# Rooms handed out by age, weights narrowed ahead, sums on VectorE and a first pair split from PSUM, in an attention kernel with two MLPs

## The chip, the cores and the metric

The kernel runs on one core of one Trainium2 chip. The metric is the device time of one execution in microseconds (us); lower is better. Five engines work side by side: TensorE (PE, matmuls), VectorE (DVE), ScalarE (ACT), GpSimd (POOL) and SyncE (SP), which here only starts DMA transfers. Each engine works through its own instructions in program order and waits where an operand isn't there yet.

## The reference

```python
scores = scale * q @ k.T - log(S)            # 4 batches, 12 heads, S = 448, head width 64
x = sigmoid(scores) @ v                      # attention without a row sum
x = x.transpose(0, 2, 1, 3).reshape(1792, 768)
h = x @ w_in                                 # layer 0: 768 -> 2048 -> 768
x = where(h > 0, h, exp(min(h, 0)) - 1) @ w_out
h = x @ w_in2                                # layer 1, same sizes
out = (h - tanh(h)) @ w_out2
```

The weights arrive as 64-bit floats. They are read as pairs of 32-bit integers and narrowed on the chip to 32-bit floats.

## The kernel before, in words

**Precision.** Each matmul operand is split into a rounded high part (`hi`, or a "head") and what is left (`lo`, or a "rest"), and each product is made of three matmuls: high by high, high by rest, rest by high. A head is one copy on ACT (or DVE), a rest one subtraction on DVE.

**Attention.** 24 pairs of heads go through two at a time ("n" is the pair, "m" the two). For a pair, q and k are loaded, POOL lays them side by side (`side`, L254; the first two pairs are loaded in that layout), PE transposes them (`t`), ACT and DVE copy the result from PSUM (`plain`, L352 and L354), DVE or ACT makes `hi` and DVE `lo` in the tile `e` (L366, L370), PE forms the scores (`s`, L389), ACT the sigmoids (`sig`, L410), PE the product with v (`pv`, L416). Beside it the second weights of layer 0 are loaded, narrowed (`p_load`, `p_narrow`, L617 to L624), summed and stored to memory.

**MLP layers.** Layer i is two Strassen products in the Winograd form with seven block products P1 to P7. A step (i, g, s) is the g-th of eight groups of hidden columns and half s of the rows (512 or 384 wide). For each (i, g) two tiles of `w_in` are loaded to `first` and `second` and narrowed by three instructions (ACT, DVE, DVE); four block sums S1, S2, S4, S3 are formed (`w_sum`, L737), and then heads and rests (`w_head` L751 on ACT, `w_rest` L754 on DVE). The places W0 to W3 hold them: W0 is for P1 and P2, W1 (from S1 and S2) for P5 and P6. Between step (i, g-1, 1) and (i, g, 0) lies what is called passage (i, g) here. In a step, ACT copies P1, P5 and P6 out of PSUM (`snap` s1, s5, s2, L834), DVE adds the rest (`h_add`, L839), ACT and DVE form the activation (`g_a`, `g_b`, `g_c`) and DVE the sums for the next product (`g_sum`, L884), and SP stores the seven forms (`f_store`, L888). `first_out` (layer 0) and `strassen_out` (layer 1) form the second product: they load the forms back (`og_load`, L946) and the weights' forms (`ow_load`, L935), split them (L949, L953, L938, L942), and multiply (L977) in the order P1, P5, P6, P3, P7, P2, P4. During `first_out` the second weights of layer 1 are loaded and narrowed in the rooms R1a and R1b in turn and kept in memory (`ahead`; L606, L617 to L624, L632). At the end of `first_out`, R1a and R1b also take up the layer's output (`o2_out`, L995).

**Rooms.** Snaps, activations and loaded forms stand in numbered rooms t0 to t25, parts of the tiles `t`, `second`, `spare`, `R1b` and others. `ring` gives out the room of a list that was given out longest ago, as the program is written, and a user waits until the former users are done:

```python
slot_of[key] = t = min(slots, key=lambda t: (used.get((kind[0], t), 0), slots.index(t)))
used[kind[0], t] = turns[0]
```

The lists are in `RINGS`: "g0" for the loads of `first_out` (rooms 23 to 25, then 0 to 6), "s10" for the snaps of steps (1, 0, s=0), "s11" for s=1, "sa" for step (0, 0, 1).

**Order.** PE's order in the MLP part is written out (`sequence`). The other engines' order is planned while the program is built, in `Sched`: of the ready operations the one that can start first by the planner's costs comes next, then the one with the lower rank (`when` for attention, from `PHASES`, `SHIFTS` and `FIRST_PAIRS`; for the rest the time at which PE wants it). So an edit of a cost, a dependence or a rank also moves operations that it doesn't name. In the opening, `ld_first` loads q and k of pairs 0 and 1, `ld_v` v; `loads` says which come first.

Of the kernel before, what the change touches and what calls it, by code (L numbers as in the profile page):

```python
# [121 lines left out]
SHIFTS = {(0, "ldv"): -12000, (0, "sr"): ROUND - 4700, (0, "sigr"): ROUND - 3900, (0, "ldvr"): -11000}  # L122
# [4 lines left out]
def kernel(  # L127
# [20 lines left out]
    nc = tc.nc  # L148
# [46 lines left out]
    with tc.manual_schedule():  # L195
# [7 lines left out]
        def attention():  # L203
# [59 lines left out]
            def ld_first(kind, i):  # L263

                b, hp = pairs[i]
                h = slice(2 * hp, 2 * hp + 2)
                if kind == "k":
                    nc.sync.dma_start(out=kl[:, i].rearrange("p c (h d) -> p c h d", h=2), in_=k[b, h, 0:KW].rearrange("h (p c) d -> p c h d", c=3))
                else:
                    (nc.sync if i else nc.scalar).dma_start(out=ql[:, i].rearrange("p c (h d) -> p c h d", h=2), in_=q[b, h].rearrange("h (p r) d -> p r h d", r=R))  # L270

            def ld_v(m, i0, i1):
                by = nc.sync if i1 == NL else nc.scalar
                b, hp = pairs[NL * m]
                by.dma_start(
# [13 lines left out]
            def loads(m):  # L289
# [8 lines left out]
                fns = {"ldv": ld_v, "ldkr": lambda m: ld_rests(0, m), "ldvr": lambda m: ld_rests(1, m), "ldkfirst": lambda i: ld_first("k", i), "ldqfirst": lambda i: ld_first("q", i)}  # L298
                for x, key in enumerate(todo):
# [5 lines left out]
                    sch.moves[key] = {"ldv": 650 * (args[-1] - args[-2]) if kind == "ldv" else 0, "ldkr": 290, "ldvr": 290, "ldkfirst": 630, "ldqfirst": 740}[kind]  # L305
# [3 lines left out]
            def loaded(kind, n):  # L309
# [3 lines left out]
                part = [("side", n, w) for w in range(2)] if m else [("ldkfirst", i), ("ldqfirst", i)]  # L313
# [29 lines left out]
            def drain(n, x):  # L343
                by, lo, hi = parts_of(n)[x]
                at = DD * (n % 2)
# [16 lines left out]
            def hi(n):  # L362
                if hi_on(n) == "ACT":
# [95 lines left out]
            for n in range(NPR):  # L459
# [12 lines left out]
                for y, (by, c0, c1) in enumerate(parts_of(n)):  # L472
                    op(("plain", n, y), by, int(1.06 * (c1 - c0)) + 120 if by == "DVE" else int(0.83 * (c1 - c0)) + 190, drain, [("t", n), ("sr", m - 1), ("lo", n - 2)])
                op(("hi", n), hi_on(n), 600 if hi_on(n) == "DVE" else 880, hi, drained(n) + [("s", n - 2, u) for u in range(3)])
                op(("lo", n), "DVE", 1020, lo, [("hi", n)])
# [15 lines left out]
        def mlp():  # L491
# [247 lines left out]
            def sum_on(step):  # L739
                return "DVE" if step == (0, 0) else "POOL"  # L740
# [509 lines left out]
            def first_products(step):  # L1250
# [14 lines left out]
                kind, kind_r = ("sa" if step == (0, 0, 1) else f"s1{s}", "r1") if g == 0 else ("s2", "r")  # L1265
# [222 lines left out]
            for i in range(2):  # L1488
# [4 lines left out]
                for g in range(NG):  # L1493
                    first_weights(i, g)
                    for s in range(2):
                        first_products((i, g, s))
                        if (i, g, s) == (0, 0, 1):
# [66 lines left out]
```

## Time and profile before

| | us |
|---|---|
| timed runs: median of 3 | 983.35 (983.11 to 986.51) |
| the profiled execution's own time | 987.84 |
| its span, first to last instruction | 985.8 |
| PE busy in it | 969.9 |
| DVE, ACT, POOL busy | 762.4, 610.3, 107.8 |

The profile is that of one execution. Its span is what the trace shows, and some 2 us lie around it. In the views below, a row of the timeline is an instruction or a run of like ones: its start, its length, engine, line, operation, "output tile <- input tiles", shape and count, and in brackets the idle time of the engine before it with what ended that. A row of the waits sums such idle time by what was waited for.

### The profile page before, as it was taken

Reading aid. Unit: us, or ns where it says so; the run is one execution under the profiler, and the core shown is the slowest. Engines: PE = TensorE matmul, PEld = TensorE weight load, DVE = VectorE, ACT = ScalarE, POOL = GpSimd, SP = SyncE. Lnnn points to the kernel's source line nnn. Section 1 sums busy time; section 2 is a strip of 40 time slices with the busy share of each in tenths; the row PEclk is TensorE's granted clock in tenths of the full one; section 3 lists DMA queues with packets and bytes.
Section 4 is the critical chain, followed back from the end, with each engine's and each line's share of the span. In section 5 each row is a group of like instructions: output and inputs, shape, how many; then the busy total and the mean of one; then the engine's idle time right before and its main releaser. Section 6 shows DMA issues by size and latency. Waiting matters only on the chain.

```text
span 985.8 us, 15460 instructions
## 1 busy us (share of the span) xinstructions
PE 969.9 (98%) x5306; PEld 837.6 (85%) x5306; DVE 762.4 (77%) x1110; ACT 610.3 (62%) x951; POOL 107.8 (11%) x110
## 2 busy tenths in 40 slices
PE   8999999999999999999999999999999999999998
PEld 5545556989999997888999987899888999999998
DVE  3877998988888886688887997877777897656673
ACT  5889889666666675566666563444444575446652
POOL 2222311011111100000000201111111000000000
PEclk9999999999999999999999999999999999999999
DMA  8999970465555599999956525555554994455442
GB/s 244 328 318 324 329 267 17 163 211 180 189 191 189 191 303 384 381 375 375 366 173 216 162 72 189 184 186 193 195 181 158 350 318 143 131 163 177 128 143 82
DMA packets 144575, 218.61 MB, mean 222 GB/s; under 512 B 21424, under 2 KB 102896, under 8 KB 144240
## 3 DMA queue, kind: packets, MB, share of 16 engines
q1 hardware_dynamic: 143232, 217.10, 64.8%
q8 instruction: 41, 0.67, 0.3%
q10 hardware_dynamic: 1264, 0.52, 0.2%
q14 instruction: 38, 0.31, 0.1%
HBM read 142.61 MB, written 74.97 MB: 221 GB/s over the span
## 4 chain that ended last, share of the span: by engine, by line
PE 93%; DMA 3%; DVE 2%; ACT 1%; SPq 1%; issue 1%; POOL 0%; DVEq 0%; ACTq 0%; POOLq 0%
PE psa L822 13%; PE psd L822 12%; PE psx L822 10%; PE psu L977 6%; PE psv L977 6%; PE psw L977 6%; PE psa L977 6%; PE psb L977 6%; PE psb L822 6%; PE pv L416 5%; PE psy L977 5%; PE sps L389 4%; PE psx L977 3%; PE psd L977 1%; DMA R1a<-in_moe_w_in_dram 1%; PE pv L427 1%
## 5 line engine op out<-in xcount | busy, mean ns | idle before, releaser
L949 ACT ACTIVATE XB<-t 128x384 fp32r<-128x384 f32 (+1 forms) x111 | 62.5, 563 | 40.0 <-PE psw L977 12.2
L953 DVE TENSOR_TENSOR XB<-t,XB 128x384 fp32r<-128x384 f32 (+1 forms) x111 | 68.4, 626 | 12.6 <-ACT XB L949 12.1
L737 POOL TENSOR_TENSOR second<-second 128x384 f32<-128x384 f32 x15 | 17.7, 1180 | 549.3 <-DMA t<-x_forms 212.5
L410 ACT ACTIVATE an<-sps,bias 128x896 f32<-128x896 f32 x72 | 70.7, 1024 | 9.7 <-PE sps L389 9.2
L949 ACT ACTIVATE XB<-spare 128x512 fp32r<-128x512 f32 (+1 forms) x72 | 41.0, 572 | 27.2 <-PE psw L977 9.6
L416 PE MATMUL pv<-an,vl 128*64 128x448 f32 x288 | 56.8, 544 | 0.0
L822 PE MATMUL psa<-XB,W 128*128 128x512 f32 x192 | 55.2, 396 | 0.0
L389 PE MATMUL sps<-e 64*128 64x448 f32 x432 | 52.5, 380 | 1.1 <-ACT plain L352 0.7
L389 PEld LDWEIGHTS sps<-e 64*128 64x128 f32 x432 | 37.6, 184 | 16.9 <-issue 7.8
L416 PEld LDWEIGHTS pv<-an,vl 128*64 128x64 f32 x288 | 19.5, 136 | 36.5 <-issue 30.7
L953 DVE TENSOR_TENSOR XB<-spare,XB 128x512 fp32r<-128x512 f32 (+1 forms) x72 | 44.1, 621 | 7.8 <-ACT XB L949 7.7
L254 POOL COPY first<-raw_qk 128x384 f32<-128x384 f32 (+1 forms) x44 | 36.4, 852 | 93.8 <-DMA raw_qk<-in_k_dram 74.2
L977 PE MATMUL psu<-XB,XB 128*128 128x384 f32 (+1 forms) x192 | 46.3, 348 | 0.0
L977 PE MATMUL psv<-XB,XB 128*128 128x384 f32 (+1 forms) x192 | 46.2, 348 | 0.0
L977 PE MATMUL psw<-XB,XB 128*128 128x384 f32 (+1 forms) x192 | 46.2, 348 | 0.0
L822 PEld LDWEIGHTS psa<-XB,W 128*128 128x128 f32 x192 | 36.8, 192 | 7.9
L851 ACT ACTIVATE spare<-t 128x512 f32<-128x512 f32 (+1 forms) x33 | 19.1, 579 | 37.0 <-DVE t L839 35.9
L822 PE MATMUL psd<-XB,W 128*128 128x512 f32 x144 | 36.8, 399 | 2.6 <-DVE W L754 2.4
L855 ACT ACTIVATE spare<-spare 128x512 f32<-128x512 f32 (+1 forms) x64 | 36.7, 576 | 1.4
L977 PE MATMUL psa<-XB,XB 128*128 128x384 f32 (+1 forms) x156 | 36.8, 347 | 0.0
L977 PE MATMUL psb<-XB,XB 128*128 128x384 f32 (+1 forms) x156 | 36.8, 347 | 0.0
L977 PEld LDWEIGHTS psu<-XB,XB 128*128 128x128 f32 x192 | 34.7, 188 | 2.1 <-DVE XB L942 0.2
(370 smaller groups left out, 2724.1 us busy)
## 6 DMA issues: line engine op xcount, KB each, us to landing
x_forms<-R1b SPq DMA_DIRECT2D x58, 256.0 KB, 2.0
first<-p_forms SPq DMA_DIRECT2D x36, 384.0 KB, 6.6
t<-x_forms SPq DMA_DIRECT2D x64, 192.0 KB, 2.9
t<-x_forms SPq DMA_DIRECT2D x47, 256.0 KB, 5.3
x_forms<-t SPq DMA_DIRECT2D x45, 256.0 KB, 2.0
x_forms<-R1b SPq DMA_DIRECT2D x58, 192.0 KB, 2.0
first<-in_moe_w_in_dram SPq DMA_DIRECT2D x14, 768.0 KB, 5.8
second<-in_moe_w_in_dram SPq DMA_DIRECT2D x14, 768.0 KB, 5.2
```

What stands on the lines that cost most here:

```text
L254: nc.gpsimd.tensor_copy(out=(ql, kl)[w][:, n % NL].rearrange("p c (h d) -> p c h d", h=2), in_=x)
L389: nc.tensor.matmul(out=ps[:, j, :S], lhsT=e[lanes, EW * kz + u * 128:EW * kz + (u + 1) * 128], rhs=e[lanes, EW * qz + KW:EW * qz + EW], st ...
L410: nc.scalar.activation(out=a, in_=T.pop(("s", n, u))[:, :, :S], func=ACTF.Sigmoid, bias=bias, scale=scale)
L416: nc.tensor.matmul(out=T["o", n][D * j:D * j + D, :S], lhsT=vl[m % NVL][:, x, 3 * j + u], rhs=a[:, j], start=False, stop=(u == 2), skip_gr ...
L427: nc.tensor.matmul(out=T["o", n][D * j:D * j + D, :S], lhsT=vrest[n // NR % 2][lanes, m % (NR // 2), j], rhs=a[lanes, j], start=True, stop ...
L737: by.tensor_tensor(out=out, in0=x, in1=y, op=op)
L822: nc.tensor.matmul(out=ps, lhsT=w[wz][:, k0:k0 + 128], rhs=xs[xz][:, kk], start=(opens and n == 0), stop=(n == 3 * KH - 1), skip_group_che ...
L851: nc.scalar.activation(out=r, in_=h, func=ACTF.Tanh)
L855: nc.scalar.activation(out=r, in_=r, func=ACTF.Exp, scale=-1.0)
L949: nc.scalar.activation(out=at_place(og_place[i, s, p, j], 0, i)[:, :HW[s]], in_=T["graw", i, s, p, j], func=ACTF.Copy)
L953: nc.vector.tensor_tensor(out=lo, in0=T.pop(("graw", i, s, p, j)), in1=f(hi), op=ALU.subtract)
L977: nc.tensor.matmul(out=T["o2", tag], lhsT=lhsT, rhs=rhs, start=(p in OPENS and j == 0 and x == 0), stop=(j == NG - 1 and x == 2), skip_gro ...
```

## The change

- **Opening.** q of pair 1 is loaded from ACT's queue, right behind q of pair 0; v of pairs 0 and 1 from SP, later in its order (`SHIFTS`: ldv of the first two pairs -4500 in place of -12000; the loads of krest for pairs 2 and 3 2500 later). For pair 0, `hi` and `lo` are formed straight from PSUM: ACT rounds the 384 columns of k to `e`, DVE the 448 of q, and two subtractions on DVE read PSUM. The copies of pair 0 to `plain` are both on ACT, the second after `lo`.
- **Passages (0, 2) and (1, 1).** The four block sums go from POOL to DVE, as at (0, 0).
- **Rooms of `first_out`.** The list "g0" is ordered at the point where it is first used: the rooms 0 to 4 whose last use is 16 or more turns back, oldest first, then 5 and 6, then the others of 0 to 4, then 23 to 25.
- **First steps of layer 1.** The snaps of steps (i, 0, 0) of layer 1 ("s10") and of (0, 0, 1) and (1, 0, 1) ("sa") get a fixed room each: s1, s5, s2 and o the first, second, third and fourth of the list; (1, 0, 1) now uses "sa" (rooms 4, 21, 22, 3).
- **Weights ahead.** The two tiles of `w_in` for passage (1, 1) are loaded, narrowed and kept during `first_out`, after the second weights, in R1a and R1b; at the passage the narrowed ones are loaded (half the bytes, nothing to narrow).

```diff
-SHIFTS = {(0, "ldv"): -12000, (0, "sr"): ROUND - 4700, (0, "sigr"): ROUND - 3900, (0, "ldvr"): -11000}
+SHIFTS = {(0, "ldv"): -4500, (1, "ldk"): 2500, (0, "sr"): ROUND - 4700, (0, "sigr"): ROUND - 3900, (0, "ldvr"): -11000}
...
-                    (nc.sync if i else nc.scalar).dma_start(out=ql[:, i].rearrange("p c (h d) -> p c h d", h=2), in_=q[b, h].rearrange("h (p r) d -> p r h d", r=R))
+                    nc.scalar.dma_start(out=ql[:, i].rearrange("p c (h d) -> p c h d", h=2), in_=q[b, h].rearrange("h (p r) d -> p r h d", r=R))
...
                     ld_first("q", 0)
+                    ld_first("q", 1)
                     nc.scalar.activation(out=warm, in_=bias, func=ACTF.Sigmoid)
-                    ld_v(0, 0, 1)
-                    todo = [("ldkfirst", 0), ("ldkr", 0), ("ldkfirst", 1), ("ldqfirst", 1), ("ldv", 0, 1, NL), ("ldvr", 0)]
+                    todo = [("ldkfirst", 0), ("ldkr", 0), ("ldkfirst", 1), ("ldv", 0, 0, 1), ("ldv", 0, 1, NL), ("ldvr", 0)]
...
             def drain(n, x):
                 by, lo, hi = parts_of(n)[x]
+                if n == 0:
+                    if x == 0:
+                        nc.scalar.activation(out=es[0][:, :KW], in_=t_flat(0)[0][:, DD:], func=ACTF.Copy)
+                    out, in_ = (plain[0][:, :DD], t_flat(0)[0][:, :DD]) if x == 0 else (kq(0)[:, KW:], t_flat(0)[1][:, :S])
+                    nc.scalar.activation(out=out, in_=in_, func=ACTF.Copy)
+                    return
...
             def hi(n):
+                if n == 0:
+                    nc.vector.tensor_copy(out=es[0][:, KW:EW], in_=t_flat(0)[1][:, :S])
+                    return
...
             def lo(n):
                 e = es[n % 2]
+                if n == 0:
+                    for a, b, ps in ((KW, EW, t_flat(0)[1][:, :S]), (0, KW, t_flat(0)[0][:, DD:])):
+                        nc.vector.tensor_tensor(out=e[:, EW + a:EW + b], in0=ps, in1=f(e[:, a:b]), op=ALU.subtract)
+                    return
...
             def sum_on(step):
-                return "DVE" if step == (0, 0) else "POOL"
+                return "DVE" if step in ((0, 0), (0, 2), (1, 1)) else "POOL"
...
-                slot_of[key] = t = min(slots, key=lambda t: (used.get((kind[0], t), 0), slots.index(t)))
+                if kind in ("s10", "sa"):
+                    t = slots[("s1", "s5", "s2", "o").index(key[2])]
+                else:
+                    t = min(slots, key=lambda t: (used.get((kind[0], t), 0), slots.index(t)))
+                slot_of[key] = t
...
-                kind, kind_r = ("sa" if step == (0, 0, 1) else f"s1{s}", "r1") if g == 0 else ("s2", "r")
+                kind, kind_r = ("sa" if step[1:] == (0, 1) else f"s1{s}", "r1") if g == 0 else ("s2", "r")
...
             def first_out():
 
+                held = {t: used["s", t] for t in range(5)}
+                old = sorted((t for t in held if held[t] <= turns[0] - 16), key=held.get)
+                RINGS["g0"] = tuple(old) + (5, 6) + tuple(sorted((t for t in held if t not in old), key=held.get)) + (23, 24, 25)
...
-                    for n in range(NF):
+                    for n, key in enumerate([("wo", 1, n) for n in range(NF)] + [("wi", 1, n) for n in (2, 3)]):
                         p, j = divmod(2 + 3 * n, NG)
-                        ahead(("wo", 1, n), (5, 2)[n % 2], 0, [("o2", 0, 0, o_order(0, 0)[p], j, 0)], True)
+                        ahead(key, (5, 2)[n % 2], 0, [("o2", 0, 0, o_order(0, 0)[p], j, 0)], True)
```

PE's own order is the same in both. Three places show what moves elsewhere.

VectorE at the start of the program, before and then changed. `pv_149` and `pv_150` hold pair 0's transposes of k and of q in PSUM, `plain_121` is their copy, `e_83` takes hi and lo of pair 0, `e_123` those of pair 1:

```order
L354 COPY plain_121<-pv_150 128x448
L366 CAST e_83<-plain_121 128x832
L370 TENSOR_TENSOR e_83<-plain_121,e_83 128x832
L366 CAST e_123<-plain_122 128x832
L370 TENSOR_TENSOR e_123<-plain_122,e_123 128x832
```

```order
L369 CAST e_83<-pv_150 128x448
L380 TENSOR_TENSOR e_83<-pv_150,e_83 128x448
L380 TENSOR_TENSOR e_83<-pv_149,e_83 128x384
L374 CAST e_123<-plain_122 128x832
L382 TENSOR_TENSOR e_123<-plain_122,e_123 128x832
```

The copy to `plain` has left VectorE, and the round and the subtraction of 832 columns have become one round of 448 and two subtractions.

VectorE at passage (0, 2), before and then changed. L839 (L854 changed) are `h_add`, L865 (L880) `g_c`, L884 (L899) `g_sum`, L754 (L769) `w_rest`; L752 is `w_sum`; W1 is the place of P5's weights, R0b here the rest of W2:

```order
L839 TENSOR_TENSOR t_2180<-t_2180,psx_2107 128x384
L865 SCALAR_TENSOR_TENSOR spare_82<-spare_82 128x384
L884 TENSOR_TENSOR R1b_2007<-t_2177,R1b_2007 128x512
L865 SCALAR_TENSOR_TENSOR R1b_2007<-spare_82,R1b_2007 128x384
L884 TENSOR_TENSOR R1b_2007<-R1b_2007,spare_82 128x384
L865 SCALAR_TENSOR_TENSOR t_2180<-spare_82,t_2180 128x384
L884 TENSOR_TENSOR R1b_2007<-t_2180,R1b_2007 128x384
L884 TENSOR_TENSOR R1b_2007<-R1b_2007,spare_82 128x384
L754 TENSOR_TENSOR W1_1769<-second_81,W1_1769 128x768
```

```order
L854 TENSOR_TENSOR t_2182<-t_2182,psx_2106 128x384
L752 TENSOR_TENSOR second_81<-second_81 128x384
L880 SCALAR_TENSOR_TENSOR spare_82<-spare_82 128x384
L752 TENSOR_TENSOR second_81<-second_81,first_80 128x384
L752 TENSOR_TENSOR first_80<-first_80,second_81 128x384 x2
L899 TENSOR_TENSOR R1b_2000<-t_2179,R1b_2000 128x512
L769 TENSOR_TENSOR W1_1767<-second_81,W1_1767 128x768
```

Between the last `h_add` and the rest of W1 stood seven instructions of the step before; now four sums and two of those seven do, and the others come behind it.

SyncE as `first_out` begins, before and then changed: `t_...`, `second` and `spare` are rooms, `x_forms00` holds the forms that are loaded back for s=0, `x_forms01` those that step (0, 7, 1) is storing. In the first piece, `x_forms01_2081<-t_3590` is the store of that step's form B21, and the last row is the load of form 0 of P5, in the room which that store reads. In the second piece, the load of form 0 of P5 is `t_3490`:

```order
L888 DMA x_forms01_2081<-t_3590 128x384
L946 DMA spare_82<-x_forms00_1982 128x512
L946 DMA t_3609<-x_forms00_1982 128x512
L606 DMA R1a_3615<-in_moe2_w_out_dram 128x1536
L946 DMA t_3622<-x_forms00_1982 128x512
L946 DMA spare_82<-x_forms00_1982 128x512
L935 DMA first_80<-p_forms_357 128x768
L946 DMA t_3639<-x_forms00_1982 128x512
```

```order
L961 DMA second_81<-x_forms00_1984 128x512
L961 DMA t_3490<-x_forms00_1984 128x512
L903 DMA x_forms00_1984<-R1b_2000 128x512
L961 DMA second_81<-x_forms00_1984 128x512 x2
L903 DMA x_forms00_1984<-t_3508 128x512
L950 DMA first_80<-p_forms_442 128x768
L903 DMA x_forms01_2080<-spare_82 128x384
L903 DMA x_forms00_1984<-R1b_2000 128x512
```

The load has moved ahead of all stores of step (0, 7, 1), to right behind the fourth load for P1, in room t1.

## Rows read from the trace of the kernel before

**Rows 1.** Page, part 1: busy us (share of the span) xinstructions.
```profile
PE 969.9 (98%) x5306; PEld 837.6 (85%) x5306; DVE 762.4 (77%) x1110; ACT 610.3 (62%) x951; POOL 107.8 (11%) x110
```

**Rows 2.** Waits of PE: who waited for what, us in total, times, longest.
```profile
PE psd L822 <- DVE W L754: 2.4, 2, 1.3
PE psy L977 <- ACT XB L949: 2.0, 1, 2.0
...
PE psx L822 <- ACT R1b L834: 1.0, 1, 1.0
PE sps L333 <- ACT an L410: 0.9, 1, 0.9
PE sps L337 <- DMA first<-in_q_dram: 0.8, 1, 0.8
PE sps L389 <- ACT plain L352: 0.7, 2, 0.4
PE sps L333 <- POOL first L254: 0.7, 1, 0.7
PE psx L822 <- ACT t L834: 0.6, 1, 0.6
```

**Rows 3.** Windows: stretch, us, busy by engine; PEclk is the granted clock.
```profile
381.60:385.10 3.50, 3.50 (x8) 2.83 (x9) 1.47 (x2) 1.94 (x4) 0.00 (x0) 0.51 1.05 406
603.50:607.00 3.50, 3.50 (x10) 2.73 (x9) 2.03 (x4) 1.12 (x2) 0.00 (x0) 0.51 0.75 204
```

**Rows 4.** Timeline of the opening: start us, us, engine, instruction, idle before.
```profile
6.70 0.62 DVE L354 COPY plain<-pv 128x448 f32<-128x448 f32 x1 [5.77 <-PE pv L337]
...
8.07 1.03 DVE L370 TENSOR_TENSOR e<-plain,e 128x832 fp32r<-128x832 f32 x1
...
9.15 1.88 PE L389 MATMUL sps<-e 64*128 64x448 f32 x16 [0.34 <-DVE e L370]
...
13.60 0.55 PE L333 MATMUL sps<-ident,first 128*128 128x128 f32 x3 [0.69 <-POOL first L254]
```

**Rows 5.** Timeline in attention, ACT.
```profile
61.63 0.92 ACT L617 ACTIVATE XB<-XB 128x768 f32<-128x768 f32 x1 [2.15 <-DMA XB<-in_moe_w_out_dram]
```

**Rows 6.** Timeline at passage (0, 2), DVE and POOL.
```profile
207.23 1.20 DVE L865 SCALAR_TENSOR_TENSOR spare<-spare 128x384 f32<-128x384 f32 x1
...
209.39 1.34 POOL L737 TENSOR_TENSOR first<-first,second 128x384 f32<-128x384 f32 x1
...
211.66 0.55 DVE L865 SCALAR_TENSOR_TENSOR t<-spare,t 128x384 f32<-128x384 f32 x1
...
213.31 0.95 DVE L754 TENSOR_TENSOR W<-second,W 128x768 fp32r<-128x768 f32 x1
```

**Rows 7.** Chain of waits as first_out begins: start us, us, what.
```profile
367.73 6.34 DMA x_forms<-t
...
374.09 6.08 DMA t<-x_forms
```

**Rows 8.** Timeline at passage (1, 1).
```profile
588.28 0.48 ACT L834 ACTIVATE R1b<-psx 128x384 f32<-128x384 f32 x1
...
597.48 1.35 POOL L737 TENSOR_TENSOR first<-first,second 128x384 f32<-128x384 f32 x1
...
601.62 0.95 DVE L754 TENSOR_TENSOR W<-second,W 128x768 fp32r<-128x768 f32 x1
```

**Rows 9.** Tile R1a in first_out: its loads (ns, first and last start), landing times.
```profile
L606 SPq DMA_DIRECT2D R1a<-in_moe_w_out_dram x8: 332/333/1392, 370.9 to 477.2; - x8
...
DMA to landing us min/median/max: 6.3/7.8/9.9
```

**Rows 10.** Windows in first_out; the last three columns are PEclk, DMA share, GB/s.
```profile
386.00:490.00 104.00, 104.00 (x472) 87.66 (x471) 81.86 (x117) 65.11 (x99) 0.00 (x0) 1.00 1.02 373
490.00:506.00 16.00, 16.00 (x95) 16.00 (x94) 13.37 (x18) 9.41 (x15) 0.00 (x0) 1.00 0.70 240
```

**Rows 11.** Timeline near the end of first_out: the first output in R1a.
```profile
505.15 0.49 ACT L995 ACTIVATE R1a<-psu 128x384 f32<-128x384 f32 x1
```

More of the change, by code (lines that the diff above doesn't have):

```diff
@@ L269, in ld_first @@
                 else:
-                    (nc.sync if i else nc.scalar).dma_start(out=ql[:, i].rearrange("p c (h d) -> p c h d", h=2), in_=q[b, h].rearrange("h (p r) d -> p r h d", r=R))
+                    nc.scalar.dma_start(out=ql[:, i].rearrange("p c (h d) -> p c h d", h=2), in_=q[b, h].rearrange("h (p r) d -> p r h d", r=R))
             def ld_v(m, i0, i1):
-                by = nc.sync if i1 == NL else nc.scalar
                 b, hp = pairs[NL * m]
-                by.dma_start(
+                nc.sync.dma_start(
                     out=vl[m % NVL][:, i0:i1].rearrange("p i (h c) d -> p (i h) (c d)", h=2),
@@ L294, in loads @@
                     ld_first("q", 0)
+                    ld_first("q", 1)
                     nc.scalar.activation(out=warm, in_=bias, func=ACTF.Sigmoid)
-                    ld_v(0, 0, 1)
-                    todo = [("ldkfirst", 0), ("ldkr", 0), ("ldkfirst", 1), ("ldqfirst", 1), ("ldv", 0, 1, NL), ("ldvr", 0)]
-                fns = {"ldv": ld_v, "ldkr": lambda m: ld_rests(0, m), "ldvr": lambda m: ld_rests(1, m), "ldkfirst": lambda i: ld_first("k", i), "ldqfirst": lambda i: ld_first("q", i)}
+                    todo = [("ldkfirst", 0), ("ldkr", 0), ("ldkfirst", 1), ("ldv", 0, 0, 1), ("ldv", 0, 1, NL), ("ldvr", 0)]
+                fns = {"ldv": ld_v, "ldkr": lambda m: ld_rests(0, m), "ldvr": lambda m: ld_rests(1, m), "ldkfirst": lambda i: ld_first("k", i)}
                 for x, key in enumerate(todo):
@@ L304, in loads @@
                     }.get(kind, [])
-                    sch.moves[key] = {"ldv": 650 * (args[-1] - args[-2]) if kind == "ldv" else 0, "ldkr": 290, "ldvr": 290, "ldkfirst": 630, "ldqfirst": 740}[kind]
+                    sch.moves[key] = {"ldv": 650 * (args[-1] - args[-2]) if kind == "ldv" else 0, "ldkr": 290, "ldvr": 290, "ldkfirst": 630}[kind]
                     sch.op(key, "SP", {"ldkr": 1300, "ldvr": 1300}.get(kind, 600), lambda fn=fns[kind], args=args: fn(*args),
@@ L312, in loaded @@
                     return [("ldv", m, 0, NL)] if m else [("ldv", m, i, i + 1)]
-                part = [("side", n, w) for w in range(2)] if m else [("ldkfirst", i), ("ldqfirst", i)]
+                part = [("side", n, w) for w in range(2)] if m else [("ldkfirst", i)]
                 return part + ([("ldkr", n // 2)] if n % 2 == 0 else [])
@@ L472, in attention @@
                 for y, (by, c0, c1) in enumerate(parts_of(n)):
+                    if n == 0:
+                        sch.op(("plain", 0, y), "ACT", (820, 560)[y], lambda y=y: drain(0, y), [[("t", 0)], [("lo", 0)]][y], when("plain", 0) + 1000 * y)
+                        continue
                     op(("plain", n, y), by, int(1.06 * (c1 - c0)) + 120 if by == "DVE" else int(0.83 * (c1 - c0)) + 190, drain, [("t", n), ("sr", m - 1), ("lo", n - 2)])
-                op(("hi", n), hi_on(n), 600 if hi_on(n) == "DVE" else 880, hi, drained(n) + [("s", n - 2, u) for u in range(3)])
-                op(("lo", n), "DVE", 1020, lo, [("hi", n)])
+                op(("hi", n), hi_on(n), 600 if hi_on(n) == "DVE" else 880, hi, (drained(n) if n else [("t", 0)]) + [("s", n - 2, u) for u in range(3)])
+                op(("lo", n), "DVE", 1020 if n else 1180, lo, [("hi", n)] + ([] if n else [("plain", 0, 0)]))
                 for u in range(3):
@@ L1496, in mlp @@
                         first_products((i, g, s))
-                        if (i, g, s) == (0, 0, 1):
+                        if (g, s) == (0, 1):
                             scratch_free[0] += turn_of["t21"] + turn_of["t22"]
```

## The prediction

> **What bounds the kernel now.** I read the page's busy times first. PE works 969.9 of 985.8 us [rows 1]: less than 16 us can be won by waiting less, since PE's instructions and their order stay as they are. DVE at 77% and ACT at 62% matter only where PE stands for them. So the second view is PE's waits [rows 2]. The reader is to see that the idle time is a short list of single events, each with its releaser, and that two rows (DVE W and ACT XB) hold 4.4 us. The third view is the granted clock around the two longest stops: for 3.5 us behind each it is 0.51, the lower of its two levels (1.2 of 2.4 GHz) [rows 3]. PE had stood 2.0 us shortly before the first and 1.3 us before the second [rows 2]; from 386 to 506 it shows full clock [rows 10]. At half clock 3.5 us do 1.7 us less work, so each such stop costs its length and 1.7 us more. I then followed every wait to its place in the timeline and asked whether the change takes its cause away and what would be late next.
>
> **Part A, the opening.** Today DVE copies 448 columns from PSUM at 6.70, rounds and subtracts 832 columns until 9.10, and the scores go on at 9.15 [rows 4]. After the change DVE's chain is a round of 448 columns from PSUM and two subtractions of 448 and 384. No row has a subtraction from PSUM of this kind here; I price it by the copy of 448 from PSUM, 0.62, and by 1.03 × 448/832 = 0.55 from the subtraction of 832. That gives 6.70 + 0.62 + 0.62 + 0.55 = 8.5, or 0.6 us earlier. ACT's rounding of k lies beside DVE's. q of pair 1, which PE missed for 0.8 us [rows 2], is issued some 2 us earlier from ACT's queue and then no longer ends last. What SP loses there (two loads of v and that q) lets the loads for pairs 2 and 3 go out earlier, and with them POOL's layout copies, for which PE waited 0.7 us at 13.60 [rows 2, 4]. Behind this, v lands later, but it is wanted by PE only after the sigmoids, some 5 us after I expect it. Sum 0.6 + 0.7 = 1.3, and I take 1.2. Bounds: 0.6 if only the first term comes, 1.8 if all three waits (0.8 + 0.3 + 0.7) go.
>
> **Part B, passage (0, 2).** POOL's four sums end at 209.39 + 1.34 = 210.7; W1's rest runs 213.31 to 214.26, and PE waits 1.1 us for it [rows 2, 6], so it was wanted at 213.2. On DVE a sum of 384 columns should cost what other operations of that shape cost when POOL is quiet, 0.55; four are 2.2. They are not all extra: beside POOL's sums the same `g_c` took 1.20 in place of 0.55 [rows 6], and three operations were stretched like this, by some 2 us in all. From the first stretched row: 207.23 + four sums 2.2 + one `g_c` 0.55 + one `g_sum` of 512 (0.55 × 512/384 = 0.73) + the rest 0.95 = 211.7, 1.5 us before it is wanted. The stop goes whole: 1.1. Queued behind the sums on DVE are five operations of the step before. They feed stores and forms that PE doesn't read until `first_out`, so their delay is free. Bounds 0.5 to 1.1.
>
> **Part C, the rooms of first_out.** The chain of waits as `first_out` begins is a store of 6.34 us from room t0, then at once a load of 6.08 into it, landing at 380.17 [rows 7]; ACT and DVE split it and PE starts P5 2.0 us late [rows 2]. In the change this load uses t1, free since step (0, 7, 0) and stands in SP's order some 18 us earlier. Even with the longest landing of R1a's loads in this stage, 9.9 us [rows 9], it comes before 370. Next late are the loads of forms 1 and 2 of P5, now in the rooms t5 and t6, freed by the last `g_c` operations; by SP's order they land some 7 us before PE wants them. Gain 2.0, and 1.7 for the clock.
>
> **Part D, first steps of layer 1.** At (1, 0, 1) the snap s1 was to use a room in R1b that was still held as operands' source; ACT made it at 588.28 [rows 8], and PE stood 1.0 and then 0.6 us for the snaps [rows 2]. With s1 in room t4 the snap can follow its product. Gain 1.6; 1.0 if s2 stays late.
>
> **Part E, passage (1, 1).** The same as B, with more: the narrowing of two tiles goes (on ACT 0.92 each, as in [rows 5], and two instructions each on DVE), and the tiles to load are half as long. POOL's sums end at 598.8, W1's rest at 602.6 [rows 8], and PE waits 1.3 us [rows 2]. On DVE the sums need 2.2 in place of POOL's last one alone at 1.35, and they can start as soon as both tiles have landed, which no narrowing holds up; the rest should end several us before it is wanted. Gain 1.3, and 1.7 for the clock. The work isn't gone: two loads of 768 KB and two stores of 384 KB, 2.3 MB, go to `first_out`. There DMA is full until 490 (share 1.02 at 373 GB/s) and then falls to 0.70 [rows 10]. 2.3 MB at 373 GB/s are 6.2 us. ACT and DVE have room (65 and 82 of 104 us busy). What is queued behind these DMAs on SP are loads of forms, for which PE never waited from 386 to 506: it is busy through all of it [rows 10]. R1a, though, is wanted for the first output at 505.15 [rows 11], and PE's P6 needs the bank that this output empties and comes right behind it, as yet without a wait. By SP's new order the last store from R1a stands beside loads that went out at about 492 before; with up to 8 us to land that is 500. I take no cost, and carry the other case below.
>
> **Part F, attention.** Three stops of 0.9, 0.4 and 0.35 us come from sigmoids and copies that are late [rows 2]. ACT stood 2.15 us at 61.63 for a tile of weights in front of them [rows 5]. In the changed order of ACT the three narrowings that waited for DMA stand behind the sigmoids. It is a side effect of the new plan and may meet the next late tile. Bounds 0 to 1.6; I take the middle, 0.8.
>
> **How the numbers follow.** Idle: 1.2 + 1.1 + 2.0 + 1.6 + 1.3 + 0.8 = 8.0. Clock: 2 × 1.7 = 3.4. Sum 11.4. Against the profiled execution's own time 987.84 (span 985.8, about 2 around it) that gives 976.4. The median of the timed runs is 4.5 us lower, and nothing says that these stops are what differs; the same 11.4 from 983.35 give 971.95. Forecast **972**.
>
> **The rivals.**
>
> First, the clock is not given back. In the rows the clock falls right after these stops and nowhere else inside the MLP part, so I count it. But the tie is by place alone; the two falls could have another cause, or be missing in the timed runs. Then the gain is 8.0: **975**. By a rule of the Trainium skill (TensorE: Matmul & The Clock Gate, section "HAM oscillation — how this bites in real kernels") it takes idle gaps longer than any of these to throw the clock back, so closing these stops would return nothing; the rows speak against that. Chance 0.13.
>
> Second, attention meets another late tile. A late tile cost ACT up to 2.15 us [rows 5], and that goes straight to PE, whose scores start as soon as `plain` is there. With A at 0.6 and F at -2 the gain is 11.4 - 0.6 - 2.8 = 8.0: **975** as well. Chance 0.17.
>
> Third, the extra tiles come late. R1a was filled 8 times from 370.9 to 477.2 [rows 9], a cycle of 15.2 for load, narrowing and store. If the cycle doesn't shorten, the ninth load starts at 492.4 and its store lands at 507.6; P6 is some 2 us late. The cycle starts from an early read of R1a by PE, and C takes 3.7 us out of PE's time behind that, so measured on PE's time the store may be 3.7 later still and P6 6 us late. With one clock fall 3.8 to 7.5 are lost: 976 to 979.5, say **978**. Chance 0.18.
>
> Fourth, slower: the same two rooms, and the DMA's full queues stretch the cycle by all the added traffic. The store then lands at 507.6 + 6.2, on PE's time 3.7 later, about 517.5. P6 is 12 us late, with a fall of the clock nearly 14: 983.35 - 11.4 + 13.7 = **985.7**, and 989 without the 3.4 of the clock. The change loses more than it gives once that store lands after about 515. Against it: the loads of forms, which PE didn't wait for there, can give way to the cycle's DMAs, and DMA falls to 0.70 from 490 [rows 10]. Chance 0.05.
>
> Fifth, the change doesn't do what it says: a cover that I see is not real, as when DVE's sums make an `h_add` late that PE waits for in P4. DVE is almost full at the passages, so B and E could turn to 0 and with them one clock fall: 972 + 4.1 = **976**; 0.05.
>
> The forecast keeps 0.42. A 0.5% difference is about what a measurement of this kernel can tell; that is below 978.4 or above 988.3. Faster takes the forecast, the first two rivals, the fifth and half of the third, 0.42 + 0.13 + 0.17 + 0.05 + 0.09 = 0.86, as far as the prices hold. Prices of stops in a planned order are easily missed, so I give 0.80, 0.15 and 0.05. The range goes from 967.5, all upper bounds (A 1.8, F 1.6) and some more waits gone, to 980.5, which takes in the third rival's long end and leaves out the fourth.
>
> **What would show it.** In the profile of the changed kernel: scores of pair 0 at about 8.5 and no wait of PE for POOL at 13; the waits for DVE W gone at both passages, DVE's L752 rows at 0.55 and the `g_c` beside them at 0.55 too; P5 of `first_out` without a stop and the clock at 1.00 through it; snap s1 of (1, 0, 1) right behind its product; PE's busy time about 966.5, that is 3.4 less, all from the clock. Wrong would be: a row of PE's waits for R1a or R1b around 500, for DVE W still, or new waits for `plain` between 60 and 150; a clock of 0.5 where PE didn't stand; or a DVE sum of 1 us or more.

## The result

The changed kernel ran at 975.04 us in the median of four runs (973.46 to 975.85), the kernel before beside it at 983.23 of four; the ratio is 0.9909, with a 95% interval of 0.9883 to 0.9934. The forecast was 972, the range 967.5 to 980.5. In a later comparison the changed kernel had 974.83 of 5 runs and the kernel before 984.48 of 11 (ratio 0.9898, 0.988 to 0.9916). In all later comparisons together the kernel before ran 70 times at 981.0 to 988.7 with a median of 985.0: the few runs that the prediction started from lay low. Against the 974.9 of the changed kernel's nine runs the change is worth about 10 us, less than the 11.4 of the sum and more than the first comparison's 8.2.

The page of the changed kernel, part 1, answers [rows 1]: busy us (share of the span), instructions. The span is 971.7.

```profile
PE 964.0 (99%) x5306; PEld 835.2 (86%) x5306; DVE 763.4 (79%) x1118; ACT 606.6 (62%) x953; POOL 101.0 (10%) x102
```

PE's waits in the changed kernel, which answer [rows 2] (who waited for what, us in total, times, longest):

```profile
...
PE pv L334 <- DMA krest<-in_k_dram: 0.6, 1, 0.6
PE psa L837 <- DVE t L854: 0.5, 1, 0.5
PE psd L837 <- ACT first L849: 0.4, 1, 0.4
PE sps L401 <- ACT plain L357: 0.4, 1, 0.4
```

All eight rows of [rows 2] are gone but for `plain`, which is now one wait of 0.4 at 39, and three small waits are new: `krest` in the opening, and `psa` and `psd` at the start of layer 0, which no step of the prediction had. The windows that answer [rows 3], behind the two places where PE stood (stretch, us, busy by engine, then the granted clock, DMA share, GB/s):

```profile
375.00:380.00 5.00, 5.00 (x23) 4.13 (x23) 3.46 (x5) 4.51 (x9) 0.00 (x0) 1.00 1.05 404
590.00:596.00 6.00, 6.00 (x29) 4.94 (x28) 5.27 (x11) 2.13 (x4) 0.00 (x0) 1.00 0.86 263
```

PE is busy through both, at full clock. PE's busy time fell by 5.9, where the prediction's sign asked for 3.4, and by 2.4 against a second profile of the kernel before (966.4, below), in which the clock fell at no stop; so not all of the fall in busy time is the clock. Passage (0, 2), to be read beside [rows 6] (timeline: start, length, instruction):

```profile
205.55 0.55 DVE L752 TENSOR_TENSOR second<-second 128x384 f32<-128x384 f32 x1
206.02 0.55 DVE L880 SCALAR_TENSOR_TENSOR spare<-spare 128x384 f32<-128x384 f32 x1
...
208.53 0.96 DVE L769 TENSOR_TENSOR W<-second,W 128x768 fp32r<-128x768 f32 x1
...
210.63 2.20 PE L837 MATMUL psd<-XB,W 128*128 128x512 f32 x9
```

A sum and a `g_c` both take 0.55, as priced; the rest of W1 ends at 209.49, 1.1 us before PE's P5, which now runs in one piece.

**Where the time went, stretch by stretch.** PE's instructions stand in the same order in every kernel here, so the start of one matmul in two traces can be compared. The table has the time between seven such marks in the profile of each kernel; the kernels are those of the experiments below.

| kernel | start of pair 1's scores | to P1 of (0,0,0) | to P3 of (0,0,1) | to P3 of (0,2,0) | to P5, j=1, of first_out | to P1 of (1,0,0) | to P3 of (1,1,0) | to the end |
|---|---|---|---|---|---|---|---|---|
| before, first profile | 14.70 | 142.59 | 20.75 | 40.08 | 167.01 | 183.47 | 39.40 | 377.8 |
| before, second (b_again) | 14.61 | 141.68 | 20.75 | 40.11 | 165.00 | 183.46 | 37.79 | 377.8 |
| changed | 12.86 | 141.08 | 22.27 | 38.49 | 162.60 | 183.27 | 33.60 | 377.6 |
| changed, second (a_again) | 14.17 | 141.15 | 22.28 | 38.61 | 162.60 | 183.27 | 33.60 | 377.6 |
| c_only | 14.76 | 140.64 | 20.75 | 39.99 | 162.60 | 183.27 | 37.83 | 377.9 |
| sums_only | 14.50 | 140.21 | 20.75 | 38.47 | 164.85 | 183.46 | 35.74 | 377.8 |
| ahead_only | 14.62 | 140.58 | 20.75 | 40.09 | 167.50 | 184.25 | 36.60 | 379.7 |
| d_only | 15.17 | 139.98 | 20.75 | 40.00 | 165.31 | 183.47 | 49.45 | 378.5 |
| d_ahead | 14.71 | 140.09 | 20.75 | 40.16 | 165.32 | 184.24 | 33.59 | 381.6 |
| no_ahead | 12.73 | 140.06 | 22.27 | 38.50 | 162.60 | 183.27 | 46.39 | 377.8 |
| no_de | 14.04 | 140.23 | 22.27 | 38.50 | 162.60 | 183.27 | 35.74 | 377.9 |
| no_open | 14.72 | 140.92 | 20.75 | 38.35 | 162.60 | 183.27 | 33.60 | 377.6 |
| dve01 | 13.72 | 140.59 | 20.97 | 38.57 | 162.60 | 183.27 | 33.60 | 377.9 |
| no_open_dve01 | 14.67 | 140.05 | 20.75 | 38.38 | 162.60 | 183.27 | 33.60 | 377.6 |

In the MLP part the same code gives the same figure to 0.3 us, mostly to 0.1, in whichever kernel it stands, unless the clock falls or a DMA takes longer. In the opening and in attention it doesn't: two profiles of the changed kernel differ by 1.3 us at the first mark. Only the mean of several profiles says something there: the first mark stands at 14.7 on average in the nine profiles with the old opening (14.5 to 15.2) and at 13.5 in the five with the new one (12.7 to 14.2).

### The profile page after: what moved, and what is told of

Its sections match the earlier page's. It is cut to its first block, busy times and chain, and to the rows that moved or that the text cites. A ratio compares the mean times of both kernels' runs of the same rounds, so it can differ in the third digit from the quotient of the medians.

```text
span 971.7 us, 15458 instructions
## 1 busy us (share of the span) xinstructions
PE 964.0 (99%) x5306; PEld 835.2 (86%) x5306; DVE 763.4 (79%) x1118; ACT 606.6 (62%) x953; POOL 101.0 (10%) x102
## 4 chain that ended last, share of the span: by engine, by line
PE 96%; DVE 1%; DMA 1%; ACT 1%; issue 0%; SPq 0%; DVEq 0%; ACTq 0%
PE psa L837 13%; PE psd L837 12%; PE psx L837 10%; PE psv L992 7%; PE psu L992 7%; PE psw L992 7%; PE psa L992 6%; PE psb L992 6%; PE psb L837 6%; PE pv L428 5%; PE sps L401 5%; PE psy L992 5%; PE psx L992 3%; PE psd L992 1%; PE pv L439 1%; PE sps L412 1%
## 5 line engine op out<-in xcount | busy, mean ns | idle before, releaser
L422 ACT ACTIVATE an<-sps,bias 128x896 f32<-128x896 f32 x72 | 70.5, 1020 | 12.1 <-PE sps L401 11.8
L752 POOL TENSOR_TENSOR second<-second 128x384 f32<-128x384 f32 x13 | 14.6, 1120 | 546.0 <-DMA spare<-p_forms 209.9
L992 PEld LDWEIGHTS psv<-XB,XB 128*128 128x128 f32 x192 | 34.7, 188 | 1.9
L992 PEld LDWEIGHTS psw<-XB,XB 128*128 128x128 f32 x192 | 34.7, 188 | 1.9
```

Of the source, the lines that this page charges most:

```text
L422: nc.scalar.activation(out=a, in_=T.pop(("s", n, u))[:, :, :S], func=ACTF.Sigmoid, bias=bias, scale=scale)
L752: by.tensor_tensor(out=out, in0=x, in1=y, op=op)
L992: nc.tensor.matmul(out=T["o2", tag], lhsT=lhsT, rhs=rhs, start=(p in OPENS and j == 0 and x == 0), stop=(j == NG - 1 and x == 2), skip_gro ...
```

## The experiments

Each has the kernel before beside it on the same chip. "before" in the results is its median there.

**The kernel before, again (b_again).** No edit.

> The kernel before, unchanged, to see how its own runs differ. Theory 1 (the clock falls belong to the kernel): every run shows the mean clock of the first profile, 0.997, and the spans lie together; then 987.84 against a median of 983.35 has another cause. Theory 2 (the falls come and go): runs near 986 to 988 show 0.997, runs near 982 to 983 show 0.998 to 1.0, about 1.7 us per fall, so that closing the two stops returns less in the median than in the first pair of profiles.

985.02 of 12 runs against 985.57 of 26; 981.0 to 988.1 over both. Theory 2 held on the average. The mean clock of a run goes from 0.995 to 1.0, and over the 70 runs of this kernel the mean time falls with it: 982.4 at 1.0 (7 runs), 984.7 at 0.998 (23), 986.7 at 0.995 (8), some 0.8 us for each 0.001. Single runs don't lie on that line: the 22 runs at 0.996 go from 983.2 to 988.7. The second profile's waits and windows:

```profile
PE psd L822 <- DVE W L754: 2.3, 2, 1.3
PE psy L977 <- ACT XB L949: 1.6, 1, 1.6
PE pv L416 <- ACT an L410: 1.5, 1, 1.5
```

```profile
378.00:386.00 8.00, 6.30 (x27) 4.99 (x27) 6.35 (x9) 7.20 (x12) 0.00 (x0) 1.00 1.05 405
601.00:607.00 6.00, 6.00 (x28) 4.98 (x27) 2.37 (x4) 2.30 (x4) 0.00 (x0) 1.00 0.94 279
```

The same two places stop PE, for 1.6 and 1.3 us, and behind them the clock stays at 1.00 this time. The three stops of part F between 62 and 79 [rows 2, 5] are not there at all, and one of 1.5 us stands at 22 instead, where ACT waited 2.8 us for another tile of weights.

**The rooms of first_out alone (c_only).**

```diff
+                held = {t: used["s", t] for t in range(5)}
+                old = sorted((t for t in held if held[t] <= turns[0] - 16), key=held.get)
+                RINGS["g0"] = tuple(old) + (5, 6) + tuple(sorted((t for t in held if t not in old), key=held.get)) + (23, 24, 25)
```

> The kernel before with the room order of first_out alone. Both theories: PE's wait of 2.0 us for the first form of P5 is gone. Theory 1: 983.2 - 2.0 - 1.7 = 979.5, and the profile shows the clock at 1.00 through P5 and one fall left, at passage (1, 1). Theory 2: 981.2 in the median. Rival (the stop only moves): another wait for a loaded form of P5, and 983.

980.04 (before 985.57; ratio 0.9955, 0.994 to 0.997). The stretch up to P5 has 162.60 in place of 165.00, so the stop is worth 2.4 without the clock, and it is gone, with no wait in its place. The timed gain of 5.5 (3.0 to 5.9 by the interval) agrees with 2.4 and the clock, which rose from 0.997 to 0.9986 on the mean: by 0.8 us for each 0.001 that is 1 us, so 3.5 together, near the interval's low end. Theory 1 asked for a fall of the clock at (1, 1). The stop of 1.3 is there, the fall isn't. The one fall of this profile stands at 8.7 to 12.1, in the opening, behind PE's wait of 1.1 for q of pair 1.

**Sums on VectorE alone (sums_only).**

```diff
-                return "DVE" if step == (0, 0) else "POOL"
+                return "DVE" if step in ((0, 0), (0, 2), (1, 1)) else "POOL"
```

> The kernel before with the sums of passages (0, 2) and (1, 1) on VectorE and nothing else. If POOL's sums are what made both stops, PE's waits for DVE W are gone: 983.2 - 2.4 = 980.8, and 979.1 with the clock's fall behind (1, 1). If at (1, 1) the narrowing of the two tiles sets the end, its stop of 1.3 us stays at 0.5 us or more and the gain is 1.1 to 1.9: 981.3 to 982.1.

980.39 (ratio 0.9946, 0.9925 to 0.9967). No wait for DVE W is left. Passage (0, 2) gives 1.6 (40.11 to 38.47) and (1, 1) 2.05 (37.79 to 35.74), with the narrowing still in place: to close either stop it is enough to take the sums from POOL.

**Weights ahead alone (ahead_only).**

```diff
-                    for n in range(NF):
+                    for n, key in enumerate([("wo", 1, n) for n in range(NF)] + [("wi", 1, n) for n in (2, 3)]):
...
-                        ahead(("wo", 1, n), (5, 2)[n % 2], 0, [("o2", 0, 0, o_order(0, 0)[p], j, 0)], True)
+                        ahead(key, (5, 2)[n % 2], 0, [("o2", 0, 0, o_order(0, 0)[p], j, 0)], True)
```

> The kernel before with the two tiles for passage (1, 1) narrowed ahead during first_out and nothing else; the sums stay on POOL. If the narrowing sets the end at (1, 1), the stop of 1.3 us and the fall of the clock are gone: 983.2 - 1.3 to 3.0 = 980.2 to 981.9. If POOL's sums set it, the sums start earlier by the narrowing's time (3 us of VectorE) all the same and the stop goes too. Price of the extra traffic: no new wait of PE between 386 and 530 (theory of the forecast), or one of 2 to 6 us at P6 near 506 (the rival).

986.3 (ratio 1.0015, 1.0 to 1.003): no gain. The stop at (1, 1) closes, with the sums still on POOL, so that stop needed the narrowing and the sums together. But the new plan of the other engines loses the gain again, in waits of PE behind `first_out` and in layer 1's steps. In this profile the stop at P5 is longer too, 2.7 us, and the clock falls there. Its waits, of which the last three rows are new:

```profile
PE psy L977 <- ACT XB L949: 2.7, 1, 2.7
...
PE psa L822 <- DVE t L839: 1.0, 1, 1.0
PE psu L977 <- DVE XB L942: 0.5, 1, 0.5
...
PE psx L822 <- DVE spare L839: 0.4, 2, 0.2
```

None is at P6, near 506: the extra tiles don't come late.

**The fixed rooms alone (d_only).** The edits of the change in `ring`, in `kind` and in the condition behind `first_products`, and nothing else.

> The kernel before with the fixed rooms for the first steps of layer 1 alone. Forecast's part D: PE's waits for the snaps at (1, 0, 1), 1.0 and 0.6, are gone and nothing else moves: 985.4 - 1.6 = 983.8, too little for the timed runs, so the profile decides. Rival: with s1 early, s5 or s2 is late instead and a wait of 0.5 or more stays.

994.78 (before 984.48; ratio 1.0103, 1.0082 to 1.0123). The snap waits are gone, as part D asked, but neither expectation had what came in their place, a new wait that is far longer.

```profile
PE psa L822 <- ACT e L751: 7.3, 1, 7.3
...
PE psa L822 <- DVE t L839: 2.2, 1, 2.2
```

PE stands 7.3 us for the head of W0 at (1, 1). The list gives snaps s5 and s2 the rooms 21 and 22, the last third of `first`. That is also where the narrowing of that passage's tiles works, so it waits for these rooms' last store. The clock has a part in the 10 us: it is at 0.5 for 3.4 us behind the wait of 2.2 and for 10.2 around the one of 7.3, and its mean over the six runs is 0.993 where the kernel before has 0.9974.

**The changed kernel again (a_again).** No edit.

> The changed kernel, unchanged, beside many runs of the kernel before. The kernel before ran at 981 to 988 with a mean clock of 0.995 to 1.0 (38 runs, median 985.4). Theory 2 (clock falls come and go with the two stops, and the change closes both): the changed kernel shows 1.0 in nearly all runs, its runs lie within 3 us, and the median gain against many runs of before is 10 to 11, more than the 8.2 of the first few runs. Theory 1 as forecast: 8 + 3.4 = 11.4. If the true gain is 8: a median of 977.

974.83 (before 984.48; ratio 0.9898). Four runs show a clock of 1.0, one 0.999, and the runs lie within 2 us. The gain of 9.7 is just under the 10 to 11 that theory 2 asked for. Its interval, 8.3 to 11.8, takes that in but the 11.4 of theory 1 as well; what speaks for theory 2 is the clock.

**Without the opening (no_open).** The changed kernel with the loads, `hi`, `lo` and copies of the first pair as before.

> The changed kernel without its opening: q, k, v loads, hi and lo of the first pair as before; all else as changed. The forecast's part A: 1.2 us slower than the changed kernel in the opening, and part F: the three stops between 62 and 79 come back, 0.8 to 2.3. Rival (the stops in attention are accidents of when a tile lands; a second profile of the kernel before had none of them and one of 1.5 us at 22 instead): only the opening's 1.2 to 1.8 are lost. For the new waits of 0.4 to 0.65 at passage (0, 1): if the changed plan of the opening makes them, they are gone here.

973.57 (ratio 0.9893, 0.9875 to 0.9911): not slower than the changed kernel. The rival held for F, whose stops don't come back. It didn't hold for the opening, whose 1.2 to 1.8 should have been lost and weren't. The new opening's lead is lost again in the changed kernel itself: the stretch from P1 of (0, 0, 0) to P3 of (0, 0, 1) has 20.75 in every profile without the new opening and 22.27 or 22.28 in the four that have it (dve01, below, apart). The timeline of the changed kernel there:

```profile
165.88 1.04 POOL L752 TENSOR_TENSOR second<-second 128x384 f32<-128x384 f32 x1 [36.71 <-DMA second<-kept_wi]
...
165.96 2.17 DVE L793 TENSOR_TENSOR R1a<-R1b,R1a 128x1152 f32<-128x1152 f32 x1
...
166.88 2.12 POOL L752 TENSOR_TENSOR first<-first,second 128x384 f32<-128x384 f32 x1
...
168.78 0.73 PE L837 MATMUL psa<-XB,e 128*128 128x512 f32 x2 [0.45 <-DVE t L854]
...
176.22 0.61 PE L837 MATMUL psd<-XB,R0a 128*128 128x384 f32 x2 [0.39 <-ACT first L849]
```

POOL's sums of passage (0, 1) lie beside the sums of operands on VectorE (L793), which take 2.17 in place of 1.35, and PE's P4 and P3 wait behind them. Without the new opening the same sums lie beside each other as well, but VectorE's begins first:

```profile
165.06 1.35 DVE L778 TENSOR_TENSOR R1a<-R1b,R1a 128x1152 f32<-128x1152 f32 x1
...
165.34 1.96 POOL L737 TENSOR_TENSOR second<-second 128x384 f32<-128x384 f32 x1 [36.84 <-DMA second<-kept_wi]
```

So POOL's sums alone don't make the waits. The new opening's plan has another order on VectorE at this passage: an `h_add` has moved ahead of two operations on operands, and the sum above then begins 0.08 us behind POOL's. It begins first in all eight profiles that have the old opening and POOL's sums there, and behind POOL's in all four with the new one. Nor is it that PE comes earlier: the stretch is 22.27 wherever P1 of (0, 0, 0) starts between 152.8 and 155.3, and 20.75 with starts from 154.7 to 157.3.

**Sums of (0, 1) on VectorE too (dve01).**

```diff
-                return "DVE" if step in ((0, 0), (0, 2), (1, 1)) else "POOL"
+                return "DVE" if step in ((0, 0), (0, 1), (0, 2), (1, 1)) else "POOL"
```

> The changed kernel with the four sums of passage (0, 1) on VectorE too. In its profile POOL's sums (165.9 to 172.1) lie beside three of VectorE's sums and rests of operands that took 1.9 to 2.2 in place of 1.35, and PE waits 0.2, 0.45 and 0.4 there, which the kernel before didn't show. If the contention makes these waits, they are gone: 1.7 us faster on the trace than the changed kernel, 973.3. If VectorE is simply too full there, the four sums (2.2 us) make the waits longer: 976 or more.

973.94 (ratio 0.9895, 0.9879 to 0.9912). The waits are gone and the stretch has 20.97, with the new opening's order on VectorE: in that order it was POOL's sums that made them. Against the changed kernel's 974.83 the timed runs can't tell the difference.

**Both (no_open_dve01).** The two edits together.

> The changed kernel without its opening but with the sums of (0, 1) on VectorE. Without the opening the changed kernel was no slower (973.6 against 974.8), although its trace stood 1.9 behind at 14.7: 1.7 of that came back at the waits of passage (0, 1), which it didn't have. Theory 4 (POOL's sums of (0, 1) take the opening's gain away again; with them on VectorE it stays): its trace is 1.0 to 1.5 behind the changed kernel with those sums on VectorE, all the way to the end: 975.0 to 975.4 against 973.9. Rival (something else sets the start of layer 0, so the opening is worth nothing in either): 973.9, and the two traces meet again before 180.

973.61 (before 984.92; ratio 0.9882, 0.9857 to 0.9907). Theory 4 fell: it asked for 975.0 to 975.4. Against dve01 the trace is 0.96 behind at the first mark, 0.2 at P3 of (0, 0, 1) and level at P3 of (0, 2, 0). A stop of 0.4 for `plain` near 40 takes a part of the lead; it stands in three of the five profiles with the new opening and in none with the old. What takes the rest isn't one wait that I could name, and the stretch of attention differs by more than that from profile to profile; it stays open. It was not the POOL sums alone.

**The changed kernel without the weights ahead (no_ahead).**

> The changed kernel without the two tiles narrowed ahead; the fixed rooms and all else stay. The fixed rooms alone made the kernel before 10 us slower: in that profile the narrowing of passage (1, 1) waited for the store out of the last third of `first`, which the fixed list gives to snaps s5 and s2, and PE stood 7.3 us for W0's head. Theory 3 (the fixed rooms need the narrowing out of the way, the two parts are one): the same stop comes back here, 985 or a little less (the sums on VectorE still help). Theory of the forecast (two parts with prices of their own): 974.9 + 0 to 1.3 = 975 to 976, as the sums on VectorE alone had already closed the stop for DVE W at (1, 1).

988.47 (ratio 1.0033, 1.0015 to 1.005): 13.6 slower than the changed kernel. Theory 3 held, and more than asked. The timeline at passage (1, 1):

```profile
587.10 1.06 SPq L903 DMA_DIRECT2D x_forms<-first  x2
589.75 0.89 ACT L632 ACTIVATE first<-first 128x768 f32<-128x768 f32 x1 [2.53 <-DMA x_forms<-first]
...
593.15 4.34 PE L837 MATMUL psa<-XA,e 128*128 128x512 f32 x9 [7.26 <-ACT e L766]
```

The store of the forms from `first` goes out at 587.10; the narrowing (L632) waits for its landing, and PE 7.26 us for what comes of it. The mean clock over the runs falls to 0.9937; in the profile it is at 0.5 for 10.2 us around this stop.

**The changed kernel without fixed rooms and weights ahead (no_de).**

> The changed kernel without the fixed rooms and without the tiles ahead: opening, sums on VectorE and the rooms of first_out stay. Theory 3: the pair of parts is worth what it removes, PE's two waits for snaps at (1, 0, 1), 1.6, plus what is left at (1, 1): 974.9 + 1.6 to 2.2 = 976.5 to 977.1, and the stop for DVE W doesn't come back. By the forecast's prices: 974.9 + 1.6 + 0 to 1.3, much the same; so no_ahead and this one are read together.

976.36 (before 984.92; ratio 0.991, 0.9881 to 0.9938), just under theory 3's 976.5 to 977.1 and 1.5 slower than the changed kernel; the stretch at (1, 1) has 35.74 in place of 33.60, most of it the two waits for snaps:

```profile
PE psx L837 <- ACT R1b L849: 1.0, 1, 1.0
PE psx L837 <- ACT t L849: 0.6, 1, 0.6
```

**Fixed rooms and weights ahead, alone (d_ahead).**

> The kernel before with the fixed rooms and the tiles narrowed ahead, sums on POOL as before. Theory 3: no stop for the narrowing, the waits for snaps (1.6) and for DVE W at (1, 1) (1.3) are gone and sometimes a clock fall of 1.7 with them: 985 - 2.9 to 4.6 = 980.4 to 982. By the sum of the two alone (10 slower and 0.7 slower): 996.

982.57 (ratio 0.9976, 0.9959 to 0.9992), 0.6 above theory 3's range and far from the 996 of the sum. The stretch at (1, 1) has 33.59, as in the changed kernel, although the sums stay on POOL. With the weights ahead and the fixed rooms, the sums on VectorE add nothing at (1, 1); without them they give 2.05. Two covers lie over the same stop. The plan's losses in layer 1's later steps (381.6 in place of 377.8 to the end) take back 3.8 here.

## Why the prediction held, and where not

The range and the sign held, and all the stops that it named are closed. The sum of 11.4 against some 10 hides errors of both signs. By the table, from stretches in which the clock doesn't fall, the parts measure 1.2 in the opening (on the mean), 1.5 lost at passage (0, 1), 1.6 at (0, 2), 2.4 at P5 and 4.2 at (1, 1): together 7.9, where the forecast's idle time was 8.0. The runs agree: the kernel before at a mean clock of 1.0 takes 982.4 on average, 7.6 more than the changed kernel's 974.9. That the parts add up to the forecast is luck, since the terms for F, for the opening and for (1, 1) were each off by more than 0.7; what is left of the 10 is the clock.

**The clock: the term was mis-sized.** The forecast counted two falls of 1.7 us as part of every run. They aren't: the first profile, with both falls, was one of the longer runs of a kernel that goes from 981 to 988, in part by its clock. Of the six profiles that have the stop at P5 two show a fall there. Over 70 runs the kernel before has a mean clock of 0.9972, the changed kernel over 9 runs 0.9999; 2.7 thousandths by 0.82 us are 2.2 us, not 3.4. The first rival, nothing given back, is refuted too. By the rule of the Trainium skill that it names (TensorE: Matmul & The Clock Gate, section "HAM oscillation — how this bites in real kernels") it takes longer idle gaps than the forecast's two stops to throw the clock back. For this kernel the runs decide otherwise. The 14 profiles show ten falls while PE has work; each begins within a stop of PE or at most 1.1 us behind its end, and eight of the ten at stops of 0.55 to 2.7 us, the other two at stops of 7.3. In the changed kernel's two profiles there is none. That the median of three runs was "4.5 us lower" than the profile, which the prediction left aside, was a hint: that profile held two falls, 3.4 us, and the stops of part F.

**A third place of the clock, which no step had.** Four of the nine profiles with the old opening show a fall at about 8 to 12 us, none of the five with the new one. In the profile of no_open:

```profile
8.03:11.44 3.41, 3.41 (x20) 2.85 (x21) 2.49 (x3) 2.03 (x3) 0.71 (x1) 0.50 0.72 195
```

It cost nothing that the marks show: pair 1's scores start at 14.6 to 14.8 with the fall and at 14.5 to 15.2 without, where PE waits 0.3 to 1.1 us for POOL's copies instead. So a part of the mean clock that the change gives back had no price.

**Part C and part B were right,** 2.4 for 2.0 and 1.6 for 1.1. Each counted PE's longest wait alone; smaller ones beside it (0.2 for DVE XB at P5) went too. And a stop takes more than the idle time that the waits list: a matmul of 512 columns lasts 0.39 in its row but the next starts 0.23 behind it, so PE loses 0.16 more at each stop.

**Parts D and E: the step that failed is that each has a price of its own.** For D the prediction asked which room was late and not who else uses the room given instead. The line behind `first_products` that adds rooms 21 and 22 to what the narrowing waits for is part of the change, and E moves exactly this narrowing away. D alone costs 10 us, part of it by the clock; E alone gains nothing; the two together give 2.1 on the trace over the sums, near the 1.6 of D. E's 1.3 came from the sums on VectorE. The stretch moved by 4.2 in all (37.79 to 33.60) against 2.9 forecast for D and E without the clock.

**Part F was a mistake of reading.** The stops between 62 and 79 belonged to one execution, in which a tile came late; in the next profile of the same kernel they are gone and another is there. The words "it is a side effect of the new plan" had no row behind them. In the stretch of attention every kernel has 140 to 142.6.

**Part A came in the opening and was lost.** On the mean of the profiles the scores of pair 1 start 1.2 us sooner, as forecast, though single pairs of profiles give 1.8 and 0.4. Then 1.5 goes at passage (0, 1), where the new plan has VectorE begin just behind POOL's sums, and without the opening the changed kernel is no slower. The prediction priced the opening up to 15 us and didn't ask what its new plan does behind it. Its fifth rival named the mechanism, an `h_add` late for P4, but for VectorE's new sums at (0, 2) and (1, 1), where it didn't happen.

**The third and fourth rivals didn't come.** R1a's loads, which answer [rows 9] and [rows 11]:

```profile
L621 SPq DMA_DIRECT2D R1a<-in_moe_w_out_dram x8: 332/333/1030, 366.0 to 461.1; - x8
L621 SPq DMA_DIRECT2D R1a<-in_moe_w_in_dram x1: 383/383/383, 473.8 to 473.8; - x1
...
DMA to landing us min/median/max: 6.8/8.4/9.6
```

```profile
378.00:486.00 108.00, 108.00 (x495) 91.63 (x494) 85.61 (x125) 68.27 (x109) 0.00 (x0) 1.00 1.03 398
486.00:502.00 16.00, 16.00 (x95) 16.00 (x94) 14.94 (x19) 11.54 (x20) 0.00 (x0) 1.00 0.80 272
```

The nine loads go from 366.0 to 473.8, a cycle of 13.5 where it was 15.2. The last store from R1a goes out at 486.8, and the first output starts at 497.3 without PE waiting for P6. The longer landing of a single load (8.4 for 7.8) was made up by a shorter wait between them. The fourth rival took the 373 GB/s of [rows 10] for all that the queues can move, because the share was 1.02. In the changed kernel they moved 398 at a share of 1.03. Against no_de, which has all but parts D and E, the rate rises from 387 to 398 GB/s in the 104 us behind the start of P5 and from 263 to 325 in the 16 us after that, about 1 MB each: half of the added 2.3 MB went into the stretch that the prediction called full, and PE waited for none of it.

## What to carry to other kernels

Profile a kernel more than once before pricing its stops: those that return at the same place with the same length are the kernel's, those in a stretch that feeds on fresh DMA may be one run's. Before giving a user another room, list who else waits for that room, and test two edits that share one alone and together. An edit early in the program can reorder an engine far behind it: compare the stretches behind an edit as well as its own.

## What the runs showed of the hardware

**The clock.** Behind a stop of PE of 0.55 to 2.7 us the granted clock fell to 0.5 for 3.4 us in some executions and not in others. In the first profile of the kernel before this came behind stops of 2.0 and 1.3, in the second behind neither of 1.6 and 1.3, and stops of 1.9 (d_only, d_ahead) and 2.3 (no_ahead) show none. At the two stops of 7.3 us (d_only, no_ahead) it was at 0.5 for 10.2 us. The kernel with such stops spreads over 7 us in 70 runs (981.0 to 988.7), the changed one over 3 in 9 (973.1 to 975.9).

**POOL and VectorE.** Where a sum on POOL and an operation with two inputs from SBUF on VectorE overlap, the one that begins first keeps its time and the other ends its own time, less some 0.14, behind the first one's end. VectorE's 1152 columns took 2.17 begun 0.08 behind POOL's sum and 1.35 begun 0.28 ahead of one; POOL's 384 columns took 1.04 and 1.96 there, and 1.01 alone. VectorE's `h_add` of 512 columns, which reads one input from PSUM, kept its 0.68 beside them.
